# Taking one chunk's transposes on TensorE instead of by DMA, in a two-layer attention and gated-MLP kernel

## The chip, the cores and the metric

The kernel runs on one core of a Trainium2 chip. The metric is the device time of one execution in microseconds (us), lower is better. Before the change it took 1797.75 us, the median of three runs (1794.82 to 1799.43).

Short names: PE is the matmul engine (PEld its weight loads), ACT the activation engine, DVE the vector engine, POOL the small general engine, SP the engine whose queue issues most of the DMA. L1471 is line 1471 of the kernel's source.

## The reference

```python
x = A_x                                    # 1 x 2048 x 512, bf16
for layer in range(2):                     # the same weights twice
    x = x + A(layernorm(x))                # 32 heads of 16, ONE key and value head for all
    x = x + B(layernorm(x))
# A: p = softmax(q k^T / 4);  o = p v;  o @ wo
# B: z = gelu(x @ w_in)                    # 512 -> 1792
#    z1, z2 = halves of z;  z2 = layernorm(z2)
#    g = w_sp @ z2 + b_sp                  # "spatial": 2048 x 2048 over the tokens
#    (z1 * g) @ w_out
```

There are 32 heads x 2048 x 2048 scores in each layer. Their exponentials are the largest single piece of work. The spatial product needs z2 of *all* tokens, so a layer's attention must have ended before its last part can start.

## The kernel before

The kernel works through the tokens in chunks: 256, 256, 512, 512, 256, 128, 128 in layer 0 and 512, 512, 512, 256, 128, 128 in layer 1. `g.fin` is the number of chunks still to come, so `g.fin == 2` is the 256-token chunk, third from the end. It closes a batch of tokens whose gelu frees the "early" part of the spatial product.

**The order is planned when the kernel is built.** Each operation is given with a planned duration and its dependencies. A greedy planner inside the kernel places it in the in-order queue of one engine. The planned figures do nothing on the chip. They only decide in which order each engine meets its instructions, and that order is then fixed.

```python
def transpose(self, out, src, deps, sem, pr):                     # by DMA: 1.2 us issue, 1.4 us latency planned
    return self.sc.op("sp", lambda e: e.dma_start_transpose(out, src), 1.2, deps, pr, sem=sem, dma=131072, lat=1.4)
...
def d_act(n):                                                     # planned time of an ACT instruction
    return n * 0.8333e-3 + 0.051
```

The chunk's three hops, each of which goes by DMA or by PE:

```python
# 1. probability sums, in the routine that ends a group of heads
if g.fin:
    tr = self.transpose(self.oTt[...], self.oT[:, par, :], [ev, ...], f"oq{par}", 0.5)
    m = sc.op("dve", <reciprocal of oTt>, 0.18, [tr], 0.6)
    ...                                                           # normalise from oTt
    return
pl, ops = sc.job([(pe, 0.3)], [...])                              # last chunk: PE, through PSUM
...
# 2. projection input, project()
if g.fin > 1:
    for qt in qts:
        o = self.transpose(self.onT[:, qt, :, :], self.on[:, qt, :], norms + ..., f"ot{qt}", 0.7)
    continue
pl, (ev,) = sc.job([(pe, m * 4 * 0.06)], [<copy PSUM -> onT on DVE, or on ACT>], ...)
...
# 3. normalised rows, mixer_chunk() -> ln()
evs += self.ln(ts, ..., pr, last, g.fin == 1)                     # last argument: on PE
```

Two more parts matter. The first decides that DVE takes no exponentials while an early spatial job stands ready. The second fills PE's idle time with matmuls on zeros (`L1796`), to keep its clock up:

```python
EF = 1
WARM = 1200.0
...
# DexStream.take(): DVE's share of the exponentials
if EF and any(o.start is None and o.ready is not None and o.ready <= t for o in k.early_first):
    return None
...
# WarmStream: place a matmul on zeros where fewer columns than this were planned in the last 3.4 us
t = sc.below(f, TICK_COLS + WARM + (AHEAD if near else 0.0))
...
def fn(e):
    return e.matmul(<bank>, k.zero[:], k.zero[...], start=..., stop=...)
```

The softmax here doesn't subtract the row's maximum and nothing guards it: scores larger than these inputs give would overflow.

Of the kernel before, what the change touches and what calls it, by code (L numbers as in the profile page):

```python
# [408 lines left out]
def d_psum(n):  # L409
    return n * 1.042e-3 + 0.066  # L410
# [6 lines left out]
def d_act(n):  # L417
    return n * 0.8333e-3 + 0.051
# [27 lines left out]
class Kern:  # L446
# [207 lines left out]
    def ln(self, tiles, deps_t, dst, dst_deps, pr, urgent=False, on_pe=False):  # L654
        sc = self.sc
        n = len(tiles)
        t0 = tiles[0]
        ag = []
        for t in tiles:
            s_ = sc.op("dve", lambda e, t=t: e.bn_stats(self.st1[:, t, :], self.X[:, t, :]), 0.6, deps_t(t),  # L660
                       pr + 0.5)
            ag.append(sc.op("dve", lambda e, t=t: e.bn_aggr(self.mv1[:, t, :], self.st1[:, t:t + 1, :]), 0.13, [s_],  # L662
                            pr + 0.4))
        a = sc.op("dve" if urgent else "pool", lambda e: e.tensor_scalar(  # L664
            self.ve1[:, t0:t0 + n], self.mv1[:, t0:t0 + n, 1], LN_EPS, None, op0=ALU.add), 0.08 if urgent else 0.25, ag, pr)
        r = sc.op("pool", lambda e: e.tensor_tensor(self.rs1[:, t0:t0 + n], self.ve1[:, t0:t0 + n],
                                                    self.mhalf[:, 0:1].to_broadcast([P, n]), ALU.pow),
                  0.38 + 0.17 * n, [a, self.c_mh], pr)
        xo = []
        slots = []  # L670
        for t in tiles:
            sl = self.xn_n % 4
            self.xn_n += 1
            slots.append(sl)
            xo.append(sc.op("dve", lambda e, t=t, sl=sl: e.tensor_scalar(
                self.xn[:, sl, :], self.X[:, t, :], self.mv1[:, t, 0:1], self.rs1[:, t:t + 1], op0=ALU.subtract,
                op1=ALU.mult), 0.22, [r, self.last_xn[sl]], pr + 0.3))

        if not urgent and not on_pe:
            evs = []  # L680
            for i, (t, sl) in enumerate(zip(tiles, slots)):
                o = self.transpose(dst[:, i, :, :], self.xn[:, sl, :], [xo[i]] + dst_deps, f"xt{sl}", pr)
                self.last_xn[sl] = o
                evs.append(o)
            return evs

        def pe(e, b):
            ins = None
            for i, sl in enumerate(slots):
                for kd in range(KD):  # L690
                    k = i * KD + kd
                    ins = e.transpose(self.b16(b)[:, k * 128:(k + 1) * 128], self.xn[:, sl, kd * 128:(kd + 1) * 128],
                                      self.ident[:])
            return ins

        def cp(b):
            return dst, self.b16(b)[:, 0:n * 512].rearrange("p (t kd c) -> p t kd c", t=n, kd=KD)
        pt, (ev,) = sc.job([(pe, n * 4 * 0.06)], [dict(
            fn=lambda e, b: e.tensor_copy(*cp(b)), dur=d_psum(n * 256), prio=pr, deps=dst_deps,
            alts=[("act", lambda e, b: e.activation(*cp(b), ACTF.Copy), d_act(n * 512) + 0.1)])], xo + [self.c_id], pr)  # L700
        for sl in slots:
            self.last_xn[sl] = pt
        return [ev]


    def layer_keys(self, layer):
# [146 lines left out]
    def finish_group(self, g, pv_last):  # L853
        sc = self.sc
        nq = g.n // 128
        sc.rush = RUSH if g.fin <= RF and g.v == 1 else 0.0
        par = self.evac_n % 2
        self.evac_n += 1
        ev = sc.op("dve", lambda e: e.tensor_copy(self.oT[:, par, :], self.b32(g.pvb)), d_psum(512),  # L859
                   [pv_last, self.oT_read[par]], 0.0)  # L860
        g.evac = ev

        def pe(e, b):
            ins = None
            for i in range(4):
                ins = e.transpose(self.b16(b)[:, i * 128:(i + 1) * 128], self.oT[:, par, i * 128:(i + 1) * 128],
                                  self.ident[:])
            return ins

        def ot(b):  # L870
            return self.oTt[:, par, :] if b is None else self.b16(b)[:, 0:512]

        def rc(e, b):
            return e.reciprocal(self.rden[:, par, :, :], ot(b).rearrange(
                "p (i j r) -> p i j r", i=4, j=4)[:, :, :, DH])

        def nm(h, e, b):

            if g.n == 128:
                out = self.on[:, 0, :].rearrange("p (i j v d) -> p i j v d", j=4, v=2, d=DH)[:, :, :, g.v, :]  # L880
                s0, s1 = 0, 4
            else:
                c = 128 * (g.q.s0 + h)
                out = self.on[:, 0:nq, c:c + 128].rearrange("p i (j v d) -> p i j v d", j=4, v=2)[:, :, :, g.v, :]
                s0, s1 = h * nq, (h + 1) * nq
            return e.tensor_tensor(
                out, ot(b)[:, s0 * 128:s1 * 128].rearrange("p (i j r) -> p i j r", j=4, r=32)[:, :, :, 0:DH],
                self.rden[:, par, s0:s1, :, None].to_broadcast([P, s1 - s0, 4, DH]), ALU.mult)
        hs = range(2 if g.n == 256 else 1)
        onr = [d for qt in range(nq) for d in self.on_read[qt]]  # L890
        if g.fin:
            tr = self.transpose(self.oTt[:, par, :].rearrange("p (i r) -> p i r", i=4), self.oT[:, par, :],
                                [ev, self.rd_read[par]], f"oq{par}", 0.5)
            self.oT_read[par] = tr
            m = sc.op("dve", lambda e: rc(e, None), 0.18, [tr], 0.6)
            for h in hs:
                m = sc.op("dve", lambda e, h=h: nm(h, e, None), d_psum(256 // len(hs)), [m] + onr, 0.5)
                self.norms.append(m)
            self.rd_read[par] = m
            if g.v == 1 and g.q.s0 + g.q.ns == 4:  # L900
                norms = self.norms
                self.norms = []
                self.project(g, norms)
            return
        pl, ops = sc.job([(pe, 0.3)], [
            dict(fn=rc, dur=0.22, prio=0.6, deps=[self.rd_read[par]])] + [
            dict(fn=(lambda e, b, h=h: nm(h, e, b)), dur=d_psum(256 // len(hs)), prio=0.5,
                 deps=[d for qt in range(nq) for d in self.on_read[qt]]) for h in hs],
            [ev, self.c_id], 0.9 if g.fin <= 2 else 1.2)
        m = ops[-1]  # L910
        self.oT_read[par] = pl
        self.rd_read[par] = m
        self.norms.append(m)
        if g.v == 1 and g.q.s0 + g.q.ns == 4:
            norms = self.norms
            self.norms = []
            self.project(g, norms)
# [3 lines left out]
    def project(self, g, norms):  # L921
        sc = self.sc
        n = g.n
# [4 lines left out]
        evs = []  # L928
        for h in range((nq + 1) // 2):
# [13 lines left out]
                return (self.onT[:, qts[0]:qts[0] + m, :, :],  # L943
                        self.b16(b)[:, 0:m * 512].rearrange("p (qt c q) -> p qt c q", qt=m, c=4))
            m = len(qts)
            if g.fin > 1:
                for qt in qts:
                    o = self.transpose(self.onT[:, qt, :, :], self.on[:, qt, :], norms + list(self.onT_read), f"ot{qt}", 0.7)
                    self.on_read[qt] = [o]
                    evs.append(o)  # L950
                continue
# [3 lines left out]
                norms + [self.c_id], 0.9 if g.fin <= 2 else 1.3)  # L955
            for qt in qts:
                self.on_read[qt] = [pl]
            evs.append(ev)
        self.onT_read = []
        for qt in range(nq):  # L960
            t = g.t0 // 128 + qt
# [15 lines left out]
    def mixer_chunk(self, g):  # L977
        sc = self.sc
        n = g.n
        nt = n // 128  # L980
        T = [g.t0 // 128 + i for i in range(nt)]
        last = g.fin == 0
        pr = PR_LAST if last else (PR_SMALL if g.fin <= 2 else PRM)
        batch = [b for b in self.gelus[g.layer] if g.ci in b][0]
        evs = []
        war = list(self.xnTB_read)
        for i in range(0, nt, 2):
            ts = T[i:i + 2]
            evs += self.ln(ts, lambda t: [self.x_op[t]], self.xnTB[:, i:i + len(ts), :, :], war, pr, last, g.fin == 1)
        self.xnTB_read = []  # L990
        z2 = []
        z1 = []
# [875 lines left out]
```

## Time and profile before

The profiled run took 1798.63 us, its span is 1796.8 us, and the mean clock granted to PE was 0.995. This table cuts the span at four times of ACT's timeline: the first and last exponential of each layer.

| stage | from, to (us) | length | what sets its end |
|---|---|---|---|
| start | 0, 12.7 | 12.7 | loads |
| exponentials of layer 0 | 12.7, 851.2 | 838.5 (ACT idle 4.1) | ACT |
| gap: rest of layer 0, head of layer 1 | 851.2, 888.2 | 37.0 | PE |
| exponentials of layer 1 | 888.2, 1738.8 | 850.6 (ACT idle 10.4) | ACT |
| tail: rest of layer 1 | 1738.8, 1796.8 | 58.0 | PE |

How to read it: in the two long stages an ACT instruction more should make the kernel longer. In the gap and the tail a matmul more should. ACT takes 3556 of the 4096 blocks of 512 columns, and DVE takes 540.

### The profile page before, as it was taken

To read this page: it belongs to the slowest core of one execution; us is meant where nothing else is said; L and a number is where in the kernel's file an instruction comes from. 1 tells how busy PE (TensorE), PEld (TensorE's weight loads), DVE (VectorE), ACT (ScalarE), POOL (GpSimd) and SP (SyncE) were. 2 spreads that over 40 slices of the span, in tenths; PEclk is the share of its full clock that TensorE was granted. 3 is DMA by queue.
4 is the path that set the end of the run, shared out by engine and by line. 5 is a ranking of instruction groups with operands and counts; after the bars stand their busy time and mean duration, and the time that the engine had idled before them with its cause. 6 is when DMAs were issued, how large, how long until landed. Compare 5 with 4: busy or idle time off the path is not lost.

```text
span 1796.8 us, 29474 instructions
## 1 busy us (share of the span) xinstructions
PE 1563.1 (87%) x11691; PEld 464.7 (26%) x11773; DVE 1655.7 (92%) x2488; ACT 1722.0 (96%) x1557; POOL 56.4 (3%) x99
## 2 busy tenths in 40 slices
PE   8888888888989888999988888888888898898999
PEld 4222222212222222223532222222222222222235
DVE  8999999999999999973999999999999999999748
ACT  8999999999999999999689999999999999999983
POOL 1000000000000000000110000000000100000000
PEclk9999999999999999999999999999999999999999
DMA  4535100011010110311310001000110111203123
GB/s 148 124 77 135 54 18 4 7 30 24 10 47 27 30 48 13 77 37 54 87 36 10 4 7 19 18 7 4 30 24 13 45 30 30 51 7 77 35 82 114
DMA packets 155465, 76.14 MB, mean 42 GB/s; under 512 B 108480, under 2 KB 152128, under 8 KB 155328
## 3 DMA queue, kind: packets, MB, share of 16 engines
q1 hardware_dynamic: 153744, 74.08, 16.2%
q8 instruction: 94, 1.54, 0.4%
q14 instruction: 43, 0.35, 0.1%
q10 hardware_dynamic: 1584, 0.16, 0.1%
HBM read 31.49 MB, written 17.83 MB: 27 GB/s over the span
## 4 chain that ended last, share of the span: by engine, by line
ACT 50%; issue 20%; PE 18%; DVE 11%; POOL 1%; DMA 0%; ACTq 0%; DVEq 0%
ACT Pa L1471 49%; PE ps_all L1815 5%; PE ps_all L1196 5%; PE ps_all L1558 3%; DVE E L1667 1%; DVE st L1124 1%; PE ps_all L1286 1%; DVE st L660 1%; PE ps_all L1796 1%; DVE Pd L1698 1%; PE ps_all L998 1%; PE ps_all L1037 1%; DVE X L1291 1%; DVE E L1694 1%; DVE E L1268 1%
## 5 line engine op out<-in xcount | busy, mean ns | idle before, releaser
L1471 ACT ACTIVATE Pa<-ps_all 128x1536 bf16<-128x1536 f32 (+1 forms) x1424 | 1612.3, 1454 | 12.7 <-PE ps_all L1815 11.0
L1815 PE MATMUL ps_all<-qs,kT 32*128 32x512 bf16 x4096 | 561.0, 385 | 194.6 <-ACT Pa L1471 179.5
L1667 DVE TENSOR_SCALAR E<-ps_all 128x512 f32<-128x512 f32 x540 | 364.6, 682 | 28.4 <-PE ps_all L1815 25.7
L1796 PE MATMUL ps_all<-zero 128*128 128x512 bf16 x1065 | 331.2, 393 | 19.8 <-DVE mv L1126 6.2
L1815 PEld LDWEIGHTS ps_all<-qs,kT 32*128 32x128 bf16 x4096 | 138.6, 91 | 790.9 <-ACT Pa L1471 771.1
L1698 DVE SCALAR_TENSOR_TENSOR Pd<-E 128x1536 uint16<-128x1536 f32 x180 | 314.9, 1749 | 2.2
L1558 PE MATMUL ps_all<-Pa,V 128*32 128x512 bf16 x3556 | 316.5, 385 | 0.2 <-DVE oT L859 0.2
L1558 PE MATMUL ps_all<-Pd,V 128*32 128x512 bf16 x540 | 182.6, 385 | 0.0
L1696 DVE TENSOR_TENSOR E<-E 128x1536 f16<-128x1536 f16 x180 | 171.1, 951 | 2.2
L1694 DVE TENSOR_TENSOR E<-E 128x1536 f16<-128x1536 f16 x180 | 170.8, 949 | 2.4
L1692 DVE TENSOR_SCALAR E<-E 128x1536 f16<-128x1536 uint16 x180 | 171.2, 951 | 1.5
L1196 PE MATMUL ps_all<-wsT,z2n 128*128 128x512 bf16 x568 | 160.5, 382 | 9.2 <-issue 3.8
L1796 PEld LDWEIGHTS ps_all<-zero 128*128 128x128 bf16 x1065 | 81.4, 98 | 189.8 <-issue 129.8
L1695 DVE TENSOR_SCALAR E<-E 128x1536 f16<-128x1536 f16 x180 | 98.9, 550 | 1.0
L1558 PEld LDWEIGHTS ps_all<-Pa,V 128*32 128x32 bf16 x3556 | 62.0, 94 | 114.6 <-issue 108.5
L1208 DVE TENSOR_TENSOR gp<-ps_all,gp 128x512 f16<-128x512 f32 x56 | 38.4, 688 | 52.8 <-PE ps_all L1196 52.7
L1196 PEld LDWEIGHTS ps_all<-wsT,z2n 128*128 128x128 bf16 x616 | 44.0, 97 | 78.7 <-issue 43.7
L998 PE MATMUL ps_all<-w_in_r,xnTB 128*128 128x448 bf16 x256 | 63.5, 356 | 0.9 <-DVE z2n L1009 0.4
L1037 PE MATMUL ps_all<-xnTB,w_in_r 128*128 128x512 bf16 (+2 forms) x364 | 63.1, 299 | 0.6 <-DVE z2n L1009 0.3
L664 POOL TENSOR_SCALAR ve<-mv 128x2 f32<-128x2 f32 (+1 forms) x28 | 11.8, 421 | 1395.8 <-DVE mv L662 1395.7
L1265 ACT ACTIVATE E<-ps_all 128x512 f16<-128x512 f32 (+1 forms) x52 | 26.6, 538 | 29.3 <-PE ps_all L1253 28.6
L1286 PE MATMUL ps_all<-E 128*128 128x512 bf16 x214 | 52.6, 380 | 1.8 <-DVE kT L741 0.8
(87 smaller groups left out, 947.7 us busy)
## 6 DMA issues: line engine op xcount, KB each, us to landing
wsT_scratch<-gp SPq DMA_DIRECT2D x16, 512.0 KB, 3.6
wsT<-wsT_scratch SPq DMA_DIRECT2D x8, 1024.0 KB, 5.4
z1s<-z_scratch SPq DMA_DIRECT2D x16, 448.0 KB, 3.7
z_scratch<-z1s SPq DMA_DIRECT2D x4, 896.0 KB, 5.5
z2n<-wsT_scratch SPq DMA_DIRECT2D x4, 768.0 KB, 4.8
wsT<-wsT_scratch SPq DMA_DIRECT2D x4, 768.0 KB, 5.6
X<-in_A_x_dram SPq DMA_DIRECT2D x8, 256.0 KB, 5.8
z2n<-wsT_scratch SPq DMA_DIRECT2D x2, 1024.0 KB, 8.6
```

The lines of the kernel that those rows point to most:

```text
L998: ins = e.matmul(self.b32(b)[:, 0:448], self.xnTB[:, i, kd, :], self.w_in_r[:, kd, FH + h * 448:FH + (h + 1) * 448], start=(kd == 0), stop ...
L1196: ins = e.matmul(self.b32(b), self.z2n[:, s, f * 128:(f + 1) * 128], w_[:, s - s0, :] if s - s0 < na or not spare else wsp[:, s - s0 - na, :],
L1471: return e.activation(k.Pa[:, base:base + n, :], k.b32(b0, n).rearrange("p (k q) -> p k q", k=n), ACTF.Exp, scale=SCALE)
L1558: ins = e.matmul(k.b32(u.grp.pvb)[32 * j:32 * j + 32, :], k.V[:, u.kt, :], b.slot, tile_position=(0, 32 * j), start=u.first, stop=u.last)
L1667: c = k.sc.op("dve", lambda e: e.tensor_scalar(k.ey[:, s, 512 * i:512 * (i + 1)], k.b32(j.bank.idx)[:, 0:512], E_LOG2, E_BIAS, op0=ALU.mul ...
L1692: o2 = sc.op("dve", lambda e: e.tensor_scalar(x, lo, E_X * 2.0 ** -16, E_X * E_A, op0=ALU.mult, op1=ALU.add), d_sb(n, 0.521e-3), self.ops ...
L1694: o3 = sc.op("dve", lambda e: e.tensor_tensor(w, x, x, ALU.mult), d_sb(n, 0.521e-3), [o2, self.wfree], pr)
L1695: o4 = sc.op("dve", lambda e: e.tensor_scalar(w, w, E_C, None, op0=ALU.add), d_sb(n, 0.26e-3), [o3], pr)
L1696: o5 = sc.op("dve", lambda e: e.tensor_tensor(w, w, x, ALU.mult), d_sb(n, 0.521e-3), [o4], pr)
L1698: o7 = sc.op("dve", lambda e: e.scalar_tensor_tensor(po.bitcast(U16), y, E_D, w, op0=ALU.add, op1=ALU.add), d_sb(n, 1.042e-3), [o5] + self ...
L1796: return e.matmul(k.b32(pvb if b is None else b.idx), k.zero[:], k.zero[:, None, :].to_broadcast([P, 4, P]), start=b is not None, stop=b i ...
L1815: return e.matmul(self.b32(bank), self.kT[32 * j:32 * j + 32, g.v, kt * 128:(kt + 1) * 128], self.qs[32 * j:32 * j + 32, g.q.slot, :], til ...
```

## The change

Its intent is to take three DMA latencies in a row out of the chain that ends in the early spatial jobs. The two `evs` lines keep one event for each tile of 128 tokens, now that a PE job can cover two tiles.

```diff
@@ ln() @@
         for sl in slots:
             self.last_xn[sl] = pt
-        return [ev]
+        return [ev] * n
@@ end of a group of heads @@
-        if g.fin:
+        if g.fin and g.fin != 2:
             tr = self.transpose(self.oTt[:, par, :].rearrange("p (i r) -> p i r", i=4), self.oT[:, par, :],
                                 [ev, self.rd_read[par]], f"oq{par}", 0.5)
@@ project() @@
-            if g.fin > 1:
+            if g.fin > 2:
                 for qt in qts:
                     o = self.transpose(self.onT[:, qt, :, :], self.on[:, qt, :], norms + list(self.onT_read), f"ot{qt}", 0.7)
@@ project() @@
             for qt in qts:
                 self.on_read[qt] = [pl]
-            evs.append(ev)
+                evs.append(ev)
@@ mixer_chunk() @@
-            evs += self.ln(ts, lambda t: [self.x_op[t]], self.xnTB[:, i:i + len(ts), :, :], war, pr, last, g.fin == 1)
+            evs += self.ln(ts, lambda t: [self.x_op[t]], self.xnTB[:, i:i + len(ts), :, :], war, pr, last, g.fin in (1, 2))
```

## The prediction

> **What bounds the kernel now.** I read the busy table first, then the chain that ended last, then the timeline of ACT and the windows by stage. ACT is at 96%, and half of the last-ending chain is one line, the softmax exponentials.
>
> ```profile
> PE 1563.1 (87%) x11691; PEld 464.7 (26%) x11773; DVE 1655.7 (92%) x2488; ACT 1722.0 (96%) x1557; POOL 56.4 (3%) x99
> ACT 50%; issue 20%; PE 18%; DVE 11%; POOL 1%; DMA 0%; ACTq 0%; DVEq 0%
> ```
>
> The timeline of ACT shows where ACT is not the bound: the exponentials run gapless up to 851 us (layer 0) and to 1739 us (layer 1). From there to the first exponential of layer 1 (888 us), and from 1739 us to the end, ACT only does small evacuations.
>
> ```profile
> 811.33 39.87 ACT L1471 ACTIVATE Pa<-ps_all 128x1536 bf16<-128x1536 f32 x35 [0.34 <-PE ps_all L1815]
> 888.23 1.45 ACT L1471 ACTIVATE Pa<-ps_all 128x1536 bf16<-128x1536 f32 x1
> 1694.29 44.51 ACT L1471 ACTIVATE Pa<-ps_all 128x1536 bf16<-128x1536 f32 x39 [0.44 <-PE ps_all L1815]
> 1738.81 1.28 ACT L1488 ACT_TABLE_LOAD   x1
> ```
>
> The instructions alternate between three and two blocks of 512 columns, so 39.87 us for 35 of them is 39.87 / (35 x 2.5) = 0.456 us of ACT per block (44.51 / 97.5 gives the same). The kernel splits its 4096 blocks between ACT (3556) and a polynomial on DVE (540).
>
> The windows, whose columns are PE, PEld, DVE, ACT and POOL busy, show two regimes: just before a layer's last exponential, ACT is full and DVE nearly empty; after it, PE is full.
>
> ```profile
> 1700.00:1730.00 30.00, 29.33 (x224) 9.10 (x220) 8.77 (x15) 30.00 (x28) 0.00 (x0) 1.00 0.12 38
> 1730.00:1797.00 67.00, 65.03 (x400) 33.42 (x404) 49.08 (x115) 31.52 (x48) 1.91 (x4) 1.00 0.39 115
> ```
>
> DVE is empty there because the program's own scheduler gives DVE no exponential while an "early" spatial job (second part of the spatial product, first six slices of 128 rows after the first eight) stands ready. Those jobs become ready when the third chunk from the end has been projected, normalised, multiplied by the input weights, passed through the gelu and normalised again: the chunk of this change. What of these jobs is not done before the last exponential is done after it, on a full PE:
>
> ```profile
> 1747.52 1.03 PE L1196 MATMUL ps_all<-wsT,z2n 128*128 128x512 bf16 x4
> 1751.68 5.13 PE L1196 MATMUL ps_all<-wsT,z2n 128*128 128x512 bf16 x23
> 1756.64 3.00 PE L1253 MATMUL ps_all<-z2n 128*128 128x256 bf16 x26
> ```
>
> So the start of the early jobs trades two things: earlier means a shorter PE-bound tail, but also a longer time in which DVE takes no exponentials and ACT takes them.
>
> **What the Trainium skill says.** (1) "Perfetto Trace Analysis", section "Identifying the Most-Contended Engine": take the engine with the highest occupancy, but do not trust matmul busy time as distance to the roofline. The trace agrees: ACT 96% is the bound, and PE's 87% hides slack during the exponentials (the product for the scores waits 179.5 us for ACT). (2) Same page, "Optimization Strategy": kernels with several regimes have a different contended engine in each; so it is here. (3) "VectorE: DVE Perf Modes", section "The three transpose paths": 390 ns for a 128x128 bf16 transpose on TensorE, 1309 ns by the DMA crossbar. Here a DMA transpose moves 128x512, takes 1.19 us to issue and lands after 2.4 to 2.5 us; four PE transposes take 0.39 us together. (4) Same page, "Why PSUM operands drop a tier": a PSUM operand limits DVE's fast modes. For the normalisation of the probability sums the trace shows no such loss: 424 ns from PSUM against 415 ns from SBUF for 128x256.
>
> ```profile
> L577 SPq DMA_TRANSPOSE oTt<-oT x60: 1189/1191/2255, 46.1 to 1686.4; - x60
> 1740.66 0.39 PE L866 MATMUL ps_all<-ident,oT 128*128 128x128 bf16 x4
> L886 DVE TENSOR_TENSOR on<-oTt,rden 128x256 bf16<-128x256 bf16 x44 | 18.3, 415 | 0.1
> L886 DVE TENSOR_TENSOR on<-ps_all,rden 128x256 bf16<-128x256 bf16 x4 | 1.7, 424 | 0.1
> ```
>
> **The change part by part.** The chunk has 256 tokens in both layers.
> Removed: per layer four transposes of sums, two of the projection input, two of normalised rows: 16 DMA transposes in all. DMA is not near the bound (17% of its engines' time), so what goes is latency: three hops in a row. In layer 0 the sums left PSUM at 732.65 us (cast 731.96 + 0.69) and DVE used the transposed ones at 736.2: 3.6 us, against 0.7 to 1.5 us for the PE way in the last chunk (cast at 1739.90 + 0.69, reciprocal at 1741.11). I estimate 2 us for each of three hops, about 6 us of the some 35 us from the last cast (732 us) to the gelu (767 us).
> Added: 64 PE transposes of 128 columns at about 0.06 us, 4 us of PE in all, in stretches where PE waits for ACT; four DVE copies of 128x1024 at 0.69 us, 2.7 us, where DVE has room.
> Moved: the two built programs' instruction orders tell what the scheduler makes of it, and this decides the number.
> - Layer 0: two blocks go from DVE to ACT, 2 x 0.456 = +0.9 us; two evacuations of 128x448 go from ACT to DVE, about 2 x 0.54 = -1.1 us. The early jobs do not start sooner (at score product 1906 against 1905), and after the last score product 56 instead of 54 spatial matmuls are left, 2 x 0.216 = +0.4 us (0.216 from the row above: 4.96 us from 1751.68 to 1756.64 for 23). Before the first exponential of layer 1 six closing matmuls fewer are placed, about -1 us. Sum: about -0.8 us.
> - Layer 1: six blocks go from DVE to ACT, +2.7 us; one transposed-row copy and one key copy more on ACT, early in the layer, where it has gaps of about 0.5 us: I count half of 1.4 us, +0.7 us. The early jobs start 26 score products sooner, and 44 instead of 66 spatial matmuls are left behind the last score product. Twenty of the 22 lie just ahead of the closing matmuls: 20 x 0.216 = 4.3 us. But the closing matmuls also need the last chunk's normalised rows, written at 1752.40 + 0.51 = 1752.9, with about 0.2 us for the handover; they start at 1756.64 now, so at most 3.5 us can be gained unless that chain moves as well. I take -3.7 us. Sum: -0.3 us.
> Total: -0.8 - 0.3 = -1.1 us, 1797.75 - 1.1 = about 1796.6 us.
>
> **The rivals.** First, *the tail gain in full without the exponentials' price*: if ACT had slack for eight more blocks, the change would give 4 to 6 us, 1792 us. Against it: ACT is busy 30.00 of 30.00 us in the window at 1700 us, so each block lengthens the phase. Second, *PE stalls in its order*: a PE transpose waits in PE's one queue for DVE's cast, where the DMA waited on its own queue. A late DVE would then hold up score products and starve ACT. For it: DVE is 92% busy, and its times on the chip need not be those planned. Against it: there are only 24 such transpose groups, the last chunk's groups show no idle PE before them, and the two score buffers cover about 2 us. Even 0.5 us each would be 12 us at most, 1809 us; I expect 0 to 3 us. Third, *longer holding of the two side banks*: transposes in PSUM take banks that DVE exponentials and spatial jobs need. This is in part already in the order (8 blocks fewer); the rest would show as DVE idle. Fourth, *the latency is the bound*: both layers give 6 us each, 1786 us. Against it: in layer 0 the order shows no earlier start at all.
>
> **Range and chances.** The terms are all a few us and of opposite sign; the order of layer 1 changes far beyond the chunk itself (its first gelu comes 19 ACT blocks earlier), which may add or remove small stalls of some us. Runs of the kernel before spread over 4.6 us. I give 1790 to 1804. Two per cent is 36 us, more than twelve times the total and beyond any rival: within 2% 0.95, faster 0.02, slower 0.03.
>
> **What would show it.** Right: the last exponential ends about 3 us later in all than 1738.8 us, with 3564 blocks on ACT and 532 on DVE; the time from it to the end falls from 58 to about 54 us; layer 0's last exponential stays within 1 us of 851; PE stays free of idle before the added transposes. Wrong: ACT waits for score products (now 11.0 us in total) growing by more than 3 us, with DVE or a transpose as PE's releaser (the second rival); a tail still at 58 us, so that the early matmuls were no bound there; or the last exponential of layer 1 coming earlier, so that blocks do not price the phase.

## The result, and the profile after

The changed kernel took 1799.33 us, the median of four runs (1797.43 to 1800.37). The kernel before took 1797.18 us in the same rounds (four runs, the three of above among them). The ratio is 1.0011, with a 95% interval of 0.9994 to 1.0028. The change is within 2%, and no difference from the kernel before is established.

The busy times and the last-ending chain of the kernel after:

```profile
PE 1577.4 (88%) x11812; PEld 467.1 (26%) x11812; DVE 1643.8 (91%) x2477; ACT 1724.7 (96%) x1558; POOL 54.1 (3%) x99
ACT 55%; issue 21%; PE 19%; DVE 5%; POOL 0%; DMA 0%; ACTq 0%; POOLq 0%
```

ACT has become busier (1724.7 against 1722.0 us) and DVE less busy. The chain lies more on ACT than before (55% against 50%). That is the exchange that the prediction described. ACT's timeline (start, length, line, instruction, count, idle time before it) gives the sizes:

```profile
851.17 1.28 ACT L1488 ACT_TABLE_LOAD   x1
...
887.54 1.45 ACT L1471 ACTIVATE Pa<-ps_all 128x1536 bf16<-128x1536 f32 x1 [1.02 <-PE ps_all L1815]
...
1672.60 71.22 ACT L1471 ACTIVATE Pa<-ps_all 128x1536 bf16<-128x1536 f32 x63 [0.81 <-PE ps_all L1815]
1743.84 1.28 ACT L1488 ACT_TABLE_LOAD   x1
```

The table load at the end of each layer marks its last exponential. It stands at 851.17 instead of 851.22 us, and at 1743.84 instead of 1738.81 us.

| stage | before | after | difference |
|---|---|---|---|
| exponentials of layer 0 | 838.5 | 838.6 | 0.0 (from the unrounded times) |
| gap | 37.0 | 36.4 | -0.6 |
| exponentials of layer 1 | 850.6 | 856.3 | +5.7 |
| tail | 58.0 | 54.1 | -3.9 |
| span | 1796.8 | 1797.9 | +1.1 |

In layer 1, ACT's exponentials became 3.0 us longer (809.72 to 812.71, six blocks more; both figures contain two table loads of 1.28 us on the same line). Its other work became 1.5 us longer: one copy of transposed rows at 1.02 us, one key copy at 0.49 us, and smaller items that cancel. Its idle time grew by 1.2 us (10.4 to 11.6).

The tail did shrink as expected. This is its PE timeline, to be read against the three PE lines of the prediction:

```profile
1756.51 1.03 PE L1196 MATMUL ps_all<-wsT,z2n 128*128 128x512 bf16 x4
1758.01 3.01 PE L1253 MATMUL ps_all<-z2n 128*128 128x256 bf16 x26 [0.48 <-DVE z2n L1134]
```

Before, the closing matmuls (L1253) began without waiting, behind the last of 27 spatial ones. Now they wait 0.48 us for the normalised rows of the last chunk. In this kernel the tail has reached the length of that chunk's own chain, so fewer early matmuls alone would shorten it no further.

The added work, in the groups of instructions of the kernel after (count, then total us and mean ns, then idle time before it; 16 of the 48 of L866 belong to the last chunks and were there before):

```profile
L866 PE MATMUL ps_all<-ident,oT 128*128 128x128 bf16 x48 | 4.7, 221 | 0.1
L886 DVE TENSOR_TENSOR on<-ps_all,rden 128x128 bf16<-128x128 bf16 x16 | 4.5, 284 | 0.1
L953 DVE COPY onT<-ps_all 128x1024 bf16<-128x1024 bf16 x2 | 1.4, 684 | 0.1
L699 DVE COPY xnTB<-ps_all 128x1024 bf16<-128x1024 bf16 x2 | 1.4, 682 | 0.0
```

The four copies cost what was estimated, 2.8 us against 2.7. The 64 transposes on PE cost more: the three groups that hold them (L866, L937, L692) grew by 3.1, 1.2 and 1.1 us, 5.4 us together against the 4 us of the estimate. There is next to no idle time just before them: PE did not stand still for them. But they had to wait in PE's one queue, as the next part shows.

**Where the shorter hops of layer 0 went.** These are lines of the timeline of all engines from the chunk's last cast of sums to its first cast of z2n; first the kernel before, then the kernel after:

```profile
731.96 0.69 DVE L859 CAST oT<-ps_all 128x512 bf16<-128x512 f32 x1
...
747.62 0.68 DVE L970 TENSOR_TENSOR X<-ps_all,X 128x512 bf16<-128x512 f32 x1
...
750.59 0.73 DVE L675 TENSOR_SCALAR xn<-X,mv,rs 128x512 bf16<-128x512 bf16 x2
...
755.24 0.55 PE L998 MATMUL ps_all<-w_in_r,xnTB 128*128 128x448 bf16 x2
...
757.80 0.61 DVE L1009 CAST z2n<-ps_all 128x448 bf16<-128x448 f32 x1
```

```profile
743.99 0.68 DVE L970 TENSOR_TENSOR X<-ps_all,X 128x512 bf16<-128x512 f32 x1
...
748.38 1.75 DVE L1698 SCALAR_TENSOR_TENSOR Pd<-E 128x1536 uint16<-128x1536 f32 x1
750.04 0.41 DVE L675 TENSOR_SCALAR xn<-X,mv,rs 128x512 bf16<-128x512 bf16 x1
...
752.67 0.61 PE L692 MATMUL ps_all<-ident,xn 128*128 128x128 bf16 x8
...
753.55 0.68 DVE L699 COPY xnTB<-ps_all 128x1024 bf16<-128x1024 bf16 x1
...
755.72 0.92 PE L998 MATMUL ps_all<-w_in_r,xnTB 128*128 128x448 bf16 x4
...
758.00 0.61 DVE L1009 CAST z2n<-ps_all 128x448 bf16<-128x448 f32 x1
```

The last cast of sums stands at 732.85 us in the kernel after, 0.9 us later than before. Two hops on, the second addition to X comes 3.6 us earlier. But the second normalised row is ready only 0.9 us earlier (750.45 against 751.32 us). Steps of DVE's exponentials now stand between the addition and that row in DVE's one queue; L1698 alone takes 1.75 us. The third hop even became longer. From that row to the first input product (L998) it takes 5.3 us by PE instead of 3.9 us by DMA: the transposes (L692) start 2.2 us after the row is ready, behind fillers and score products in PE's queue, and 1.5 us more pass between the copy (L699) and the product. The first z2n comes 0.2 us *later*. So the latency saved turned into waiting in the in-order queues of DVE and PE.

In layer 1 it was different: from the last cast of sums to the gelu it took 29.7 us instead of 39.6 us. This is why only layer 1's tail moved. Most of it comes from the second hop. From the last normalised sums to the first projection matmul (L966) it took 8.7 us before (1628.74 to 1637.40) and 2.6 us after (1628.02 to 1630.61). The two DMA transposes of that hop landed 6.7 and 6.0 us after their issue, not 2.4 to 2.5 us: three loads had been issued just ahead of them on the same queue (at 1623.7 to 1624.9 us), and from 1628 to 1636 us the DMA engines were busy for a share of 0.85. PE took up the product 1.4 us after the second landing. The average share of DMA (17%) hides such a stretch.

### The profile page after: what moved, and what is told of

Same layout as the page of the kernel before. It is cut to its first block, busy times and chain, and to the rows that moved or that the text cites. A ratio compares the mean times of both kernels' runs of the same rounds, so it can differ in the third digit from the quotient of the medians.

```text
span 1797.9 us, 29587 instructions
## 1 busy us (share of the span) xinstructions
PE 1577.4 (88%) x11812; PEld 467.1 (26%) x11812; DVE 1643.8 (91%) x2477; ACT 1724.7 (96%) x1558; POOL 54.1 (3%) x99
## 4 chain that ended last, share of the span: by engine, by line
ACT 55%; issue 21%; PE 19%; DVE 5%; POOL 0%; DMA 0%; ACTq 0%; POOLq 0%
ACT Pa L1471 52%; PE ps_all L1815 5%; PE ps_all L1196 4%; PE ps_all L1558 3%; PE ps_all L1286 2%; PE ps_all L1796 1%; PE ps_all L1253 1%; PE ps_all L998 1%; DVE st L660 1%; ACT z2n L1083 1%; ACT z1s L1079 1%; PE ps_all L1037 1%; DVE xn L675 0%; PE ps_all L966 0%; DVE E L1667 0%
## 5 line engine op out<-in xcount | busy, mean ns | idle before, releaser
L1471 ACT ACTIVATE Pa<-ps_all 128x1024 bf16<-128x1024 f32 (+1 forms) x1428 | 1615.8, 1460 | 14.8 <-PE ps_all L1815 11.1
L1667 DVE TENSOR_SCALAR E<-ps_all 128x512 f32<-128x512 f32 x532 | 359.6, 681 | 24.2 <-PE ps_all L1815 21.3
L1796 PE MATMUL ps_all<-zero 128*128 128x512 bf16 x1040 | 322.6, 393 | 16.5 <-DVE mv L1126 5.0
L1698 DVE SCALAR_TENSOR_TENSOR Pd<-E 128x1536 uint16<-128x1536 f32 (+1 forms) x178 | 310.3, 1743 | 2.1
L1196 PE MATMUL ps_all<-wsT,z2n 128*128 128x512 bf16 x616 | 170.1, 385 | 0.9 <-DVE gp L1208 0.5
L1696 DVE TENSOR_TENSOR E<-E 128x1536 f16<-128x1536 f16 (+1 forms) x178 | 168.6, 947 | 2.3
L1694 DVE TENSOR_TENSOR E<-E 128x1536 f16<-128x1536 f16 (+1 forms) x178 | 168.4, 946 | 2.4
L1692 DVE TENSOR_SCALAR E<-E 128x1536 f16<-128x1536 uint16 (+1 forms) x178 | 168.9, 949 | 1.8
L1695 DVE TENSOR_SCALAR E<-E 128x1536 f16<-128x1536 f16 (+1 forms) x178 | 97.5, 548 | 1.1
L1208 DVE TENSOR_TENSOR gp<-ps_all,gp 128x512 f16<-128x512 f32 x56 | 38.4, 686 | 57.7 <-PE ps_all L1196 57.7
L998 PE MATMUL ps_all<-w_in_r,xnTB 128*128 128x448 bf16 x256 | 64.6, 356 | 1.1 <-DVE E L1667 0.4
L664 POOL TENSOR_SCALAR ve<-mv 128x2 f32<-128x2 f32 (+1 forms) x28 | 12.4, 444 | 1396.6 <-DVE mv L662 1396.4
```

The lines of the kernel that those rows point to most:

```text
L1196: ins = e.matmul(self.b32(b), self.z2n[:, s, f * 128:(f + 1) * 128], w_[:, s - s0, :] if s - s0 < na or not spare else wsp[:, s - s0 - na, :],
L1471: return e.activation(k.Pa[:, base:base + n, :], k.b32(b0, n).rearrange("p (k q) -> p k q", k=n), ACTF.Exp, scale=SCALE)
L1667: c = k.sc.op("dve", lambda e: e.tensor_scalar(k.ey[:, s, 512 * i:512 * (i + 1)], k.b32(j.bank.idx)[:, 0:512], E_LOG2, E_BIAS, op0=ALU.mul ...
L1692: o2 = sc.op("dve", lambda e: e.tensor_scalar(x, lo, E_X * 2.0 ** -16, E_X * E_A, op0=ALU.mult, op1=ALU.add), d_sb(n, 0.521e-3), self.ops ...
L1694: o3 = sc.op("dve", lambda e: e.tensor_tensor(w, x, x, ALU.mult), d_sb(n, 0.521e-3), [o2, self.wfree], pr)
L1695: o4 = sc.op("dve", lambda e: e.tensor_scalar(w, w, E_C, None, op0=ALU.add), d_sb(n, 0.26e-3), [o3], pr)
```

## The experiments

The **exchange theory**, that of the prediction, prices an order by two counts: a block more on ACT costs 0.456 us, and a spatial matmul more left behind a layer's last score product costs 0.216 us. The **latency theory** says that shorter hops shorten a layer; the prediction put it at 6 us for three hops. The **stall theory** of the expectations says that PE, or DVE in e4 and e12, stands still at an instruction whose input is late. The **order theory** (in the expectations "tuned-order theory") says that any change of the plan moves the time by several us, whatever it was meant for. In e8, e9 and e11 "stall theory" means this too, and in e12 "order theory" means only that a fixed order can hide a longer hop. The **clock theory** ("clock-drop theory") came up on the way: PE's granted clock falls at some spots, and how often decides a few us. Both counts come from the built programs, and all kernels gave correct results. Eight of the thirteen intervals (e1 to e6, e8, e12) lie above 1. "Idle" is ACT's idle time within the two stages of exponentials.

| kernel | blocks on ACT | left in layer 0, 1 | median us | ratio to before [95%] | L0 exp / gap / L1 exp / tail | idle L0, L1 |
|---|---|---|---|---|---|---|
| before | 3556 | 54, 66 | - | 1 | 838.5 / 37.0 / 850.6 / 58.0 | 4.1, 10.4 |
| after | 3564 | 56, 44 | 1799.33 | 1.0011 [0.9994, 1.0028] | 838.6 / 36.4 / 856.3 / 54.1 | 4.5, 11.6 |
| e1 | 3559 | 56, 58 | 1799.81 | 1.0022 [1.0010, 1.0035] | 839.2 / 36.4 / 856.0 / 57.4 | 5.0, 13.2 |
| e2 | 3563 | 54, 48 | 1798.95 | 1.0015 [1.0002, 1.0027] | 836.5 / 37.0 / 854.4 / 55.6 | 2.6, 11.2 |
| e3 | 3547 | 76, 86 | 1807.86 | 1.0059 [1.0046, 1.0071] | 834.7 / 41.1 / 855.5 / 62.5 | 3.1, 13.4 |
| e4 | 3563 | 40, 56 | 1802.55 | 1.0034 [1.0020, 1.0047] | 838.4 / 36.9 / 854.6 / 55.6 | 3.1, 10.9 |
| e5 | 3559 | 56, 60 | 1815.01 | 1.0093 [1.0074, 1.0112] | 835.4 / 36.4 / 868.7 / 56.5 | 2.0, 24.9 |
| e6 | 3554 | 68, 58 | 1803.68 | 1.0039 [1.0027, 1.0051] | 837.5 / 40.0 / 854.7 / 57.0 | 4.8, 12.4 |
| e7 | 3559 | 58, 46 | 1796.03 | 0.9997 [0.9984, 1.0010] | 836.0 / 38.3 / 853.8 / 55.4 | 2.3, 11.9 |
| e8 | 3572 | 38, 46 | 1806.46 | 1.0051 [1.0039, 1.0063] | 840.6 / 36.9 / 858.3 / 55.2 | 3.7, 11.6 |
| e9 | as after | as after | 1796.58 | 1.0003 [0.9990, 1.0015] | 838.3 / 36.4 / 853.5 / 54.1 | 4.2, 9.4 |
| e10 | as before | as before | 1796.10 | 1.0000 [0.9988, 1.0013] | 837.0 / 37.0 / 850.2 / 57.7 | 2.8, 9.9 |
| e11 | as e7 | as e7 | 1797.92 | 1.0008 [0.9994, 1.0021] | 837.2 / 38.3 / 853.5 / 55.6 | 3.1, 11.4 |
| e12 | as before | as before | 1817.24 | 1.0116 [1.0102, 1.0130] | 849.3 / 37.0 / 859.5 / 57.8 | 13.4, 18.3 |

The kernel before ran beside e1 to e4 at a median of 1796.49 us, beside e5 to e8 at 1796.48, beside e9 to e12 at 1796.21. The stages are those of one profiled run, which was the slowest of its runs for e1 (1803.24) and the fastest for e2 (1797.84).

### e1 and e2: the change in one layer alone

```diff
-        if g.fin:
+        if g.fin and (g.fin != 2 or g.layer != 0):      # e2: g.layer != 1; likewise in project() and mixer_chunk()
```

> The change in layer 0 alone; layer 1 keeps its DMA transposes. Exchange theory (the time moves by 0.456 us for each block of exponentials more on ACT and by 0.216 us for each spatial matmul more that is left behind a layer's last score product; latency as such is worth nothing): the order of this kernel has 3 blocks more on ACT than before (3559 against 3556) and 56 and 58 instead of 54 and 66 matmuls left, so +1.4 - 1.3 = +0.1 us, between -1.5 and +1.5. Latency theory (each hop saved shortens its layer): -2 us or more, from layer 0 alone. Stall theory (PE waits in its order for each added transpose): +1 to +3 us, with new idle time of ACT in layer 0 and half the excess of the full change.

> The change in layer 1 alone. Exchange theory: 3563 blocks on ACT (+7, +3.2 us), 54 and 48 matmuls left (18 fewer, -3.9 us): -0.7 us, between -2.5 and +1. The last exponential of layer 1 ends some 3 us later after the first one of its layer than before, and the tail after it is 3 to 4 us shorter. Latency theory: -3 to -6 us, with the last exponential not later. Stall theory: +1 to +3 us, ACT idle for score products growing.

Measured: 1799.81 us (+3.3 on the median) and 1798.95 us (+2.5). The latency theory, which gave -2 us or more for e1 and -3 to -6 us for e2, fails on both. The exchange theory is right on the tail: 48 matmuls left in e2 give 55.6 us, 58 in e1 give 57.4 us. It is wrong on the sum. In e1 the exponentials of layer 1 take 5.4 us longer than before, although the change was left out of layer 1 and ACT takes the same 1778 blocks in it. ACT's idle time there grew by 2.8 us, the planner gave ACT the same two additional copies as in the kernel after (1.02 and 0.49 us), and as many blocks took 1.1 us longer. So these come with the new order, also where no transpose of that layer changes its engine. The stall theory gave +1 to +3 us for either run, which is near the times, but it put e1's waits in layer 0, where ACT's idle time grew by only 0.9 us. In e2 ACT's waits for score products did not grow (10.5 us against 11.0).

### e3: DVE not held back

```diff
-EF = 1
+EF = 0
```

> The kernel before, with its DMA transposes, but DVE is no longer refused exponentials while an early spatial job stands ready (one constant). Exchange theory: 9 blocks fewer on ACT (-4.1 us), 42 spatial matmuls more left behind the last score products (+9.1 us): +5.0 us, between +2.5 and +7. This moves far along the exchange in the other direction from the change and touches no transpose. Latency theory: the hops are as before, so no loss; 9 blocks fewer on ACT give -4 us. Stall theory: no PE transposes added, so -4 us too.

Measured: 1807.86 us, +11.4. This is the clearest test of the price of a matmul left over: 22 more in layer 0 made the gap 4.1 us longer (0.19 us each), 20 more in layer 1 made the tail 4.5 us longer (0.23 us each). In layer 0, six blocks fewer on ACT (1772) made its exponentials 3.8 us shorter, of which six times 0.456 us are 2.7. But those of layer 1 became 4.9 us longer with three blocks fewer (1775), which the exchange theory does not explain.

### e4: the kernel before, with its transposes planned sooner

```diff
-        return self.sc.op("sp", ..., 1.2, deps, pr, sem=sem, dma=131072, lat=1.4)
+        return self.sc.op("sp", ..., 1.2, deps, pr, sem=sem, dma=131072, lat=0.7)
```

> The kernel before, all transposes still by DMA and physically as slow, but the scheduler plans each with a landing 0.7 us sooner (2.45 us from issue, which is what the trace shows). Exchange theory: 3563 blocks on ACT (+7, +3.2 us), 40 and 56 matmuls left (24 fewer, -5.2 us): -2.0 us, between -4 and 0; so that an order like that of the change is had without any PE transpose. Latency theory: no hop is shorter, so 0, or a loss if orders planned too tight make DVE wait for landings. Stall theory: 0 to +3 us, with DVE idle for DMA landings growing above the 0.6 us of before.

Measured: 1802.55 us, +6.1, where the exchange gave about -2. With 14 matmuls fewer left in layer 0, the gap stayed at 36.9 us. So the price seems to hold in one direction only: more left-over work is paid, less need not save anything. That the last chunk's own chain is then the longer one was seen in the tail of the kernel after; for this gap it is argued. In part the stall theory was right here: DVE's waits for landings grew from 0.6 to 6.0 us, six times up to 2.5 us, now that the plan leaves less spare time for a late landing. The profiled run (1799.93 us, clock 0.996) is the second fastest of the five; the slower ones (1802.55 to 1804.96 us) had clocks of 0.991 to 0.994, and their stages are not known.

### e5 and e6: controls without any change of instructions

The kernel before is planned with one constant changed a little. No transpose changes its engine; the instructions only come in another order, and the split of the exponentials moves by three or two blocks.

```diff
-    return n * 0.8333e-3 + 0.051      # planned ACT time, e5
+    return n * 0.8333e-3 + 0.052
```

```diff
-        ... dma=131072, lat=1.4)      # planned DMA latency, e6
+        ... dma=131072, lat=1.5)
```

> Control: the kernel before with nothing changed but one planning constant, by 1 ns (the fixed part of a planned ACT instruction, 51 to 52 ns). All transposes stay on DMA, no instruction changes its kind; only the order falls out otherwise: 3559 blocks on ACT (+3, +1.4 us), 56 and 60 matmuls left (4 fewer, -0.9 us). The four runs so far lay 3 to 8 us above what the exchange theory gave. Tuned-order theory (the order of before is a picked one, and any new order loses about 3 us, by stalls and by drops of the PE clock that it happens to have more of): +2 to +6 us. Exchange theory alone: +0.5 us, between -1 and +2. If the losses came from what each edit did (transposes, DVE held back, tight planning): 0 to +1 us here.

> Second control: the kernel before, each DMA transpose planned to land 0.1 us later, nothing else. 3554 blocks on ACT (-2, -0.9 us), 68 and 58 matmuls left (6 more, +1.3 us). Tuned-order theory: +2 to +6 us. Exchange theory alone: +0.4 us, between -1 and +2.

Measured: 1815.01 us for e5 (+18.5; its six runs lie between 1805.43 and 1817.96) and 1803.68 us for e6 (+7.2). One nanosecond in the plan moved the time by more than the whole change under study did. In e6 the 14 more matmuls left in layer 0 explain 3.0 us of the longer gap; the rest lies in the exponentials of layer 1. In e5 it is nearly all there, and the windows of e5 (busy PE, PEld, DVE, ACT, POOL, then PE's clock) show what happened at 1140 us (in brackets the instructions; the last two numbers are DMA's share and GB/s):

```profile
1130.00:1140.00 10.00, 7.42 (x50) 1.95 (x51) 9.40 (x16) 8.13 (x9) 0.00 (x0) 0.86 0.34 41
1140.00:1150.00 10.00, 10.00 (x41) 1.80 (x39) 5.59 (x10) 7.26 (x6) 1.55 (x2) 0.50 0.00 0
```

PE ran at half its clock, was busy for all 10.00 us and finished only 41 matmuls. ACT was idle for 2.74 us. In the kernel before the same 10 us had a clock of 1.00 and a full ACT. The runs of e5 go with the mean clock: 1805.43 us at 0.995, and 1817.68 and 1817.96 us at 0.986.

### e7: only the projection input on PE

```diff
-            if g.fin > 1:
+            if g.fin > 2:                              # sums and normalised rows stay on DMA
```

> One part of the change alone: only the projection input of the third chunk from the end is transposed on PE, in both layers; sums and rows stay on DMA. 3559 blocks on ACT (+3, +1.4 us), 58 and 46 matmuls left (16 fewer, -3.5 us). Exchange theory alone: -2.1 us, the best of the single parts, between -4 and 0. Tuned-order theory: that plus 3 us, 0 to +3 us.

Measured: 1796.03 us (1794.84 to 1800.20), ratio 0.9997. This is the lowest ratio of all kernels run, and no gain that can be told from zero. It lands 1.6 us above its exchange estimate of -2.1. The other two parts alone were not run, so what each of the three is worth stays open.

### e8: the change with more filler matmuls

```diff
-WARM = 1200.0
+WARM = 1800.0
```

> The changed kernel, with more filler matmuls planned for PE (1337 instead of 1040), so that PE falls idle less and its clock should drop less, above all around the gelu stretches, where the trace of the change has a clock of 0.62 and 0.87 in two 10 us windows near 1390 us. 3572 blocks on ACT (+16 against before, +7.3 us), 38 and 46 matmuls left (36 fewer, -7.8 us): -0.5 us by the exchange. Clock-drop theory (the excess over the exchange is time at a lowered PE clock): the mean clock rises to 0.998 or more and the time falls to that of before, -1 to +1 us. Stall theory (the excess is waiting in a badly fitting order): +2 to +5 us at a high clock.

Measured: 1806.46 us, +10.0, at a mean clock of 0.998 to 1.000. The clock theory failed as it was put here: the clock was up and the time was up too. The fillers go through the planner, so they changed the order: eight blocks more on ACT than in the kernel after, and 38 matmuls left in layer 0 with a gap of 36.9 us all the same, as in e4. Sixteen blocks more than before are worth 7.3 us at 0.456 us each, and the two stages of exponentials became 9.8 us longer, so most of the loss is the exchange price itself.

### e9, e10 and e11: more filling with the order kept

To lift the clock without touching the order, every second filler planned in a gelu stretch of ACT, or up to 6 us after one, is issued twice: 65 matmuls more. The planner does not see them.

```diff
+        more = self.n % 2 == 0 and (k.sc.table == "gelu" or t < k.sc.t_exp + 6.0)   # t_exp: last table change
         def fn(e):
+            if more:
+                e.matmul(<bank>, k.zero[:], k.zero[...], start=..., stop=...)
             return e.matmul(<bank>, k.zero[:], k.zero[...], start=..., stop=...)
```

e9 is the kernel after with it, e10 the kernel before, e11 is e7.

> The changed kernel with its order unchanged; every second filler matmul that is planned inside a gelu stretch, or within 6 us after one, is issued twice, unknown to the planner (65 matmuls more, 14 us of PE, where PE has gaps of 1 to 1.5 us). Clock-drop theory (what the new order loses beyond the exchange is score products at half the PE clock; in the trace of the change ACT waits 3.1 us at 1390 to 1410 us and 0.8 us at 1670 us, both beside a lowered clock): the clock there stays at 1.0, those waits go, and the time falls by 1 to 3 us against the change as it is, to between -1 and +1 us against before. Stall theory (the waits come from the order itself): no gain, +1 to +3 us against before.

> The same filling in the kernel before (65 matmuls more, order unchanged). Its trace has a lowered clock at 770 to 790 us and 1670 us, but hardly a wait of ACT beside them (0.03 us at 1670). Clock-drop theory: 0 to -1 us. Stall theory: 0 to +1 us, as the doubled fillers may delay a score product. So the change should profit more than before does, if its loss is the clock.

> A version that could beat both: only the projection input on PE (e7, -0.5 us against before), with the gelu stretches filled in the same way (67 matmuls more). Clock-drop theory: -1 to -3 us against before, the fastest of the study. Stall theory: as e7, -1 to +1 us.

Measured: ratios 1.0003, 1.0000 and 1.0008. In the trace the filling does what it was made for. First the windows of the kernel after, then those of e9, at the end of layer 1's gelu stretch:

```profile
1390.00:1400.00 10.00, 8.75 (x42) 1.91 (x43) 9.35 (x15) 8.49 (x8) 1.29 (x2) 0.62 0.49 155
1400.00:1410.00 10.00, 9.85 (x64) 2.25 (x62) 7.24 (x11) 8.38 (x9) 0.00 (x0) 0.87 0.00 0
```

```profile
1390.00:1400.00 10.00, 8.93 (x64) 2.48 (x63) 9.93 (x16) 10.00 (x9) 1.29 (x2) 1.00 0.56 177
1400.00:1410.00 10.00, 9.27 (x75) 2.48 (x74) 9.34 (x15) 10.00 (x11) 0.00 (x0) 1.00 0.00 0
```

In the kernel after the clock fell to 0.62 and 0.87 and ACT lost 1.51 and 1.62 us. In e9 the clock stays at 1.00 and ACT is full. Its exponentials of layer 1 took 853.5 us instead of 856.3. So a good part of the change's longer stage in that one profile was the clock. In whole times it is 1.0003 against 1.0011, with overlapping intervals from different rounds; that is a hint and not proof. The kernel before gains nothing from the same filling (1.0000), and e11 does no better than e7. The cleanest comparison is that of e9 with e10, in the same rounds and both with a high clock: their means differ by 0.4 us, and stage by stage the change then costs +1.3 us in the exponentials of layer 0, -0.6 in the gap, +3.3 in the exponentials of layer 1 and -3.6 in the tail. No version beats both kernels.

### e12: the DMA hops made longer, with the order kept

The kernel before. Each DMA transpose of the chunk must first wait for a small extra transpose into a spare tile, which lands after 2.2 to 2.4 us.

```diff
+            if twice:                                  # only where g.fin == 2
+                self.dumps += 1
+                e.dma_start_transpose(self.dump[:], src[:, 0:128]).then_inc(self.dump_sem, 16)
+                e.wait_ge(self.dump_sem, 16 * self.dumps)
             return e.dma_start_transpose(out, src)
```

> The kernel before with its order unchanged, but each DMA transpose of the third chunk from the end is preceded by a small one (128x128, into a tile that nobody reads), and issued only when that has landed: some 2 to 3 us longer for each of three hops in both layers, unknown to the planner. This is the opposite of the change with no new order. If the length of the hops sets the end (latency theory): 3 hops x 2.5 us, +5 to +15 us over both layers. If a hop is hidden behind work that the fixed order puts ahead of its users (order theory): only what comes after the spare of some 0.7 us (planned landing 3.15 us, seen 2.4 us) can be felt, and DVE or PE stall there: 0 to +4 us, with new waits of DVE for the landings.

Measured: 1817.24 us, +21.0. The order theory, which gave 0 to 4 us, is wrong here, and the latency theory's 5 to 15 us is even exceeded. Two waits of e12 (total us, times, longest), whose lines are shifted by the edit:

```profile
ACT Pa L1480 <- PE ps_all L1824: 27.9, 39, 2.2
...
DVE rden L883 <- DMA oTt<-oT: 9.9, 8, 2.6
```

In the kernel before, DVE waited for such a landing once, for 0.6 us, and ACT waited 11.0 us for score products. While DVE waits for a late landing, what stands behind it in its queue waits too, its exponentials among it. From 735 to 775 us, around layer 0's three hops, ACT was busy for 32.6 us in e12 and for 40.0 in the kernel before. PE's clock was 0.81 to 0.85 there, against 1.00. How much of the 21 us is the landing itself and how much the lowered clock that follows is not told apart by this run.

The edit also did more than its expectation counted. Where a hop has two transposes, each waits for an extra one of its own, in one queue. From the first issue to the last landing, in layer 0, the sums' hop grew from 3.4 to 5.5 us, that of the projection input from 3.8 to 8.4 and that of the rows from 4.4 to 9.7 us. That is 12.0 us; in layer 1 it is 10.7 us by the same count. The two stages of exponentials became 10.8 and 8.9 us longer, which is about what paying the longer hops in full would give. The opposite test, a shorter hop in an unchanged order, was not run.

## Why the prediction was right

The prediction was right: 1796.6 us predicted with a range of 1790 to 1804, 1799.33 us measured, within 2%. The predicted difference of -1.1 us did not show: the medians of the same rounds differ by +2.2 us, the spans of the two profiled runs by +1.1 us, both inside the scatter of either kernel. So the main terms are confirmed in kind, and the sign of the small total is not. That the total lay inside the range owes something to luck, too: of the two controls, which change no transpose, one landed at 1803.68 us, just inside, and one at 1815.01 us, outside. By its steps:

- **What bounds the kernel.** Right. ACT sets the two stages of exponentials and PE the tail, and both moved in the direction that the exchange says.
- **Layer 0, about -0.8 us.** Right: 0.0 in the exponentials and -0.6 in the gap. The last exponential stays at 851.17 us. That it fits to the tenth is chance: with the fillers of e9 and e10 in both kernels the exponentials differ by +1.3 us. Two hops were shortened for no gain, because the queues of DVE and PE gave the time away again ahead of the gelu.
- **Layer 1, tail, -3.7 us.** Right: -3.9. The limit was also right: the closing matmuls now wait for the last chunk's rows. What the prediction had wrong is how the early jobs came sooner: it took 2 us for each of three hops, and one hop alone, that of the projection input, gave 6 us in this layer (2.6 us instead of 8.7). That fits e7, which has only this hop on PE and left 46 matmuls. Across the kernels run, 44 to 56 matmuls left give a tail of 54.1 to 55.6 us, and 58 to 60 give 56.5 to 57.4; 66 give 58.0 and 86 give 62.5.
- **Layer 1, exponentials, "+2.7 us" and copies "I count half of 1.4 us, +0.7 us".** Right in kind, too small. The exponentials measured +3.0 and ACT's other work +1.5, since both copies were paid whole. ACT's idle time, for which the sum has no term, grew by 1.2 us. Together that is +5.7 instead of +3.4 and turns -1.1 us into +1.1 us of span.
- **Cost of the transposes.** Too small: "64 PE transposes of 128 columns at about 0.06 us, 4 us of PE in all" does not follow from the row that the prediction shows (0.39 us for four); 5.4 us were measured. "0.7 to 1.5 us for the PE way" is 0.5 us for the pair it quotes (1740.59 to 1741.11). Neither moves the total.
- **Full gain without the price** (first rival). Not so: the last exponential came 5.0 us later.
- **PE stalls on its order** (second rival). Not as starving of ACT: PE's idle time before the added transposes is 0.1 us for L866, ACT's wait for score products is 11.1 us against 11.0, and all its idle time before exponentials is 14.8 us against 12.7. But a transpose did wait in PE's one queue: layer 0's third hop became 1.4 us longer by it. The "24 such transpose groups" of its bound are 12 in the changed kernel (8 of sums, 2 and 2).
- **Side banks held longer** (third rival). Not shown as idle of weight. DVE's L1208 waits longer for spatial products (54.0 to 63.0 us; the trace of the kernel before lacks some of these matmuls, so the size is rough). Spatial jobs that now run beside the exponentials, where DVE has room, would do this; that reading is argued, not tested.
- **Latency is the bound** (fourth rival). Not as a gain: neither layer gave 6 us. e12 adds what the prediction did not say, that a *longer* hop than planned costs dearly; e4 points the same way.

What the prediction missed has no effect on its number but matters more than its terms. The chance to land within 2% was put down to small terms of opposite sign. The controls show another source of some us: the planned order itself. Layer 1's exponentials take 850.6 us in the kernel before (850.2 in e10, the same order) and 853.5 us or more in each of the nine other orders, also in e3 with fewer blocks on ACT. A part of this is the blocks: with 0.456 us taken off for each block more than before, the excess is 0.2 us in e9, 1.1 to 6.3 us in the others and 16.7 us in e5. So in the change's own order with the clock kept up (e9) the block price leaves next to nothing to explain; e2 (1.1) and e7 (1.8) are near that. A likely reason for the rest is that this kernel was tuned until its order happened to be a good one, so that nearly any change starts a few us behind. That fits e1, e3, e5 and e6 best. e7 ends level, and two controls are few, so the reason stays argued.

## What to carry to other kernels

When a planner fixes the order of in-order queues, run a control before crediting a change: the old kernel with one planning constant nudged. If that moves the time by more than the change does, the change's own worth can be read only from the stages of the trace. Shortening a latency pays only where nothing else stands between its end and the next user in that engine's queue. Look there first, and look for the chain that takes over (here the last chunk's), since it caps the gain. Read a latency where it is spent: here the landing was 2.4 to 2.5 us by the median and 6.7 us in the one hop that gave the change most of its earlier start.

## What the Trainium skill lacked or had wrong

- "TensorE: Matmul & The Clock Gate", section "Why this matters for your kernels", advises to avoid throughput drops by leaving no idle gap of PE over some 3 us. That advice alone was not enough here. In the kernel after the clock fell at about 1393 us although the idle gaps marked in PE's timeline in the 13 us before were of 0.2 to 1.5 us, with PE busy 2.1 to 3.3 us of each 4 us. It then stayed at 0.50 for some 9 us, although PE was busy for all of the stretch from 1394 to 1402 us. Short gaps need not lower it either: in the kernel before, gaps of 0.2 to 1.6 us from 1387 to 1400 us left the clock at 1.00. Other parts of the page speak of short idle times too, but none says how many are too many.
- The same page, Part 1, describes two states of the clock. The trace agrees: windows of 2 us show 0.50 and 1.00 and, where a window holds a transition, a value between. That page says a warm-up count varies from run to run. What it does not say is how much the clock of a whole kernel can vary: six runs of e5 had mean clocks of 0.986 to 0.995 and times of 1805.43 to 1817.96 us.
- "VectorE: DVE Perf Modes", section "The three transpose paths", gives 1309 ns for a 128x128 DMA transpose. Here one of 128x128 (e12) took 1.12 us or more to issue and landed after 2.2 to 2.4 us, and one of 128x512 landed after 2.4 to 2.5 us, all by the median: four times the data for about the same latency. Next to loads on the same queue one of 128x512 took up to 6.7 us. The figure that a planner needs is the landing, and this section does not give it.
- None of the pages cited in this document says how much the mere order of instructions on in-order engines moves a tuned kernel: +7.2 and +18.5 us of some 1796 in the two controls.
